# The first token block in another order, with one mask load and products split into a high and a low step

## The chip, the cores and the metric

The kernel runs on one NeuronCore of a Trainium2 chip. The metric is the device time of one execution in microseconds (us), the median of several runs. The engines go by their names in the trace: PE is TensorE (matmuls and transposes), PEld its weight loads, ACT is ScalarE, DVE is VectorE, POOL is GpSimd, and SP is SyncE, which here only issues DMAs. Each engine executes its instructions in the order in which they were written, so an instruction that waits holds up all that stand behind it.

## The reference

Windowed attention is followed by two feed-forward stages, all in float32:

```
scores = scale * q @ k.T                  # 4 batches, 8 heads, 576 positions, 64 per head
mask = (rel >= 0) & (rel < 64)            # a window of 64 positions back
attn = exp(scores - max) / (sum + 1e-9)
x = (attn @ v)                            # as 2304 tokens x 512
h = x @ w_in;  g = relu(h) ** 2;  x = g @ w_out        # 512 -> 2048 -> 512
y = ((x @ w_a) * (x @ w_b)) @ w_out2                   # 512 -> 1536 -> 512
```

## The kernel before

**Numbers in two parts.** A float32 operand is split into a high part (`hi`, `xh`, `wh`, rounded to the format FP32R) and a low part (`lo`, `xl`, `wl`, what the rounding left). A product is then three matmuls, high with high, high with low and low with high, which `mm3` issues one after another for each of the four slices of the contraction.

**Weights.** The weights arrive as 64-bit words. `conv` turns one tile of 128 x 512 into `wh` and `wl`: a load on SP (`raw`, two buffers), three passes on ACT (`a`, `s`, `wh`; lines 203, 208, 230) and four on DVE (lines 211, 218, 223, 233). A unit of the first feed-forward stage is 128 of its 2048 hidden features and needs one tile of `w_in` and one of `w_out`; below they are called i0, o0 to i6, o6 for the seven units of the first pass (`G1[0]`).

**Attention.** A chunk is 128 tokens. Its steps are scores on PE (`S`), maximum on DVE (`M`, `nm`), exponential on ACT (`E`, four instructions for each half chunk), normalisation on DVE (`N`, `p`), transposes on PE (`Tr`, `ps_p`), their copy on ACT (`pT`), values on PE (`V`, `ps_o`), and the split of the result into `xh` on ACT and `xl` on DVE. For the first five chunks the mask is added on PE, by a matmul with the identity (`ident_bf`, `mask_bf`) ahead of the scores; the later ones add it on DVE from `mask_sb`. The mask has three variants: the usual one, and two for a chunk that holds the start of a batch in its first or second half.

**A unit.** `unit1` projects a block of tokens (`H`, tile `ps_in`, 12 matmuls), forms `r`, `hi` and `g` on ACT (in the first block; later `g` is on DVE) and `lo` on DVE, and adds the product with `w_out` into four accumulators (`O`, tile `acc`, 12 matmuls). The first block of 512 tokens is four chunks. In its first pass, three units are computed in halves of 256 tokens and four whole.

**What sets the order.** All steps are put in a `Plan` with an engine, an assumed cost, their dependences and a rank. `Plan.issue` walks through assumed time and takes on each engine, among the steps that are ready within 0.15 us of the first, the one of lowest rank; the program is then written in that order. A rank is given by the order of the calls `attention`, `tiles` (a pair of `conv`) and `unit1` at the end of the kernel.

Of the kernel before, what the change touches and what calls it, by code (L numbers as in the profile page):

```python
# [8 lines left out]
F32 = mybir.dt.float32  # L9
# [20 lines left out]
G2 = [range(0, 6), range(6, 12)]  # L30
C0 = 4
MASK_PE = 5
N0 = 3
NPR = NCH // 2
# [86 lines left out]
def kernel(  # L121
# [39 lines left out]
    mask_sb = mk_p.tile([P, 3, P], F32, name="mask_sb")  # L161
    mask_bf = mk_p.tile([P, 3, P], BF16, name="mask_bf")
    ident_bf = mk_p.tile([P, P], BF16, name="ident_bf")
# [133 lines left out]
    def a_scores(c):  # L297
        pool, tag = (ps_acc, "acc") if c < 2 else (ps_w, "w")
        on_pe = c < MASK_PE
        for j in range(2):  # L300
            ps = T["s", c, j] = pool.tile([P, NHP, P], F32, tag=tag, name="ps_s")
            if on_pe:
                m = mask_bf[:, mask_of(c)].unsqueeze(1).to_broadcast([P, NHP, P])
# [77 lines left out]
    def attention(c, rank):  # L381
# [8 lines left out]
        for j in range(2):  # L390
            ps = ("S", c) if c >= 2 and j else None
            add(("M", c, j), "DVE", 0.8 if on_pe else 1.45, f(a_max, j), [("S", c), old("Tr", j)], rank,
                give=None if on_pe else ps)
# [15 lines left out]
    def u_proj(name, key, t, cols):  # L409
# [3 lines left out]
        for kc in range(KC):  # L413
            c = slice(kc * P, (kc + 1) * P)
            mm3(ps, h_[:, c], l_[:, c], xh[t][:, kc, cols], xl[t][:, kc, cols], kc == 0, kc == KC - 1)

    def e_tile(tag, n, dt=F32):
        return e_p.tile([P, 512], dt, tag=tag, name=tag)[:, :n]
# [4 lines left out]
    def unit1(t, u, us, cols, rank):  # L423
# [16 lines left out]
        def g_():  # L440
            T["g", k] = e_tile("g", n)
            if t == 0 and part_1:
                nc.scalar.activation(out=T["g", k], in_=T["r", k], func=AF.Square)
# [7 lines left out]
        def lo_():  # L451
            T["lo", k] = e_tile("lo", n, F32R)
            nc.vector.tensor_tensor(out=T["lo", k], in0=T["g", k], in1=T["hi", k].bitcast(F32), op=ALU.subtract)  # L453

        def out_():
            if fresh:
# [6 lines left out]
        e = 0.12 + 0.001 * n  # L463
        add(("H", k), "PE", 12 * mm_cost(n), lambda: u_proj(("H", k), ("in", u), t, cols),
            [("wlo", i), *x, ("H", k - 1) if k else None], rank, take="w")
        add(("r", k), "ACT", e, r_, [("H", k), *back(k, "g", "hi")], rank, give=("H", k))
        add(("hi", k), "ACT", e, hi_, [("r", k), *back(k, "O")], rank)
        add(("g", k), "ACT" if t == 0 and part_1 else "DVE", e, g_, [("r", k), *back(k, "lo")], rank)
        add(("lo", k), "DVE", e, lo_, [("g", k), ("hi", k), *back(k, "O")], rank)
        add(("O", k), "PE", 12 * mm_cost(n), out_,  # L470
            [("lo", k), ("wlo", o), ("O", k - 1) if k else None, *(acc_free[0] if fresh else ())], rank + 1.5)
        last_use["in", u], last_use["out", u] = ("H", k), ("O", k)
# [123 lines left out]
    def c_mask():  # L596
        nc.scalar.dma_start(out=mask_sb, in_=mask.unsqueeze(1).to_broadcast([P, 3, P]))
        make_identity(nc, ident)

    def c_masks():  # L600

        nc.gpsimd.tensor_copy(out=ident_bf, in_=ident)
        for e in range(2):
            nc.gpsimd.memset(mask_sb[e * W:(e + 1) * W, 1 + e, :W], NEG / SCALE)
        nc.gpsimd.tensor_copy(out=mask_bf, in_=mask_sb)

    add("mask", "ACT", 0.6, c_mask, [], -3, size=0.2)
    add("masks", "POOL", 1.5, c_masks, ["mask"], -3)


# [15 lines left out]

    halves = [slice(0, 256), slice(256, 512)]
    first = G1[0]
    attention(0, nxt())
    attention(1, nxt())  # L630
    for u in range(N0):
        tiles(1, u, nxt())
        if u:
            attention(1 + u, nxt())
        unit1(0, first[u], first, halves[0], nxt())
    for u in range(N0):
        unit1(0, first[u], first, halves[1], nxt())
        if u < N0 - 1:
            tiles(1, N0 + u, nxt())
    c = C0  # L640
    for j, u in enumerate(first[N0:]):
        if N0 + j >= 2 * N0 - 1:
            tiles(1, u, rank[0] - 2)
        attention(c, nxt())
        c += 1
        unit1(0, u, first, slice(0, 512), nxt())

# [96 lines left out]
```

## Time and profile before

| what | us |
|---|---|
| median of 3 runs (lowest, highest) | 942.81 (942.37, 943.44) |
| the profiled execution, its own time | 942.02 |
| its span, first to last instruction | 940.1 |
| PE busy in the span | 912.2 (97%) |
| DVE, ACT busy | 443.4, 384.5 |

The span is what the trace covers; the 1.9 us beside it lie outside the program's instructions. Of PE's idle time, 940.1 - 912.2 = 27.9 us, most lies in the first 62 us.

### The profile page before, as it was taken

The page shows a single profiled execution, that of the slowest core. Times are in us where ns is not written, and L with a number is a line of the kernel's source. Part 1 is how long each engine was busy: PE and PEld are TensorE (multiplying, and loading weights), DVE is VectorE, ACT ScalarE, POOL GpSimd, SP SyncE. Part 2 cuts the span into 40 slices and gives each one's busy share as a digit, 9 for nine tenths or more (in the row PEclk, how much of TensorE's full clock was granted, in tenths as well). Part 3 has the DMA queues.
Part 4 walks back from the last instruction along what each step waited for, and adds up shares of the span by engine and source line. Part 5 has one row for each costly group of instructions (what it writes and reads, how often), then busy time and mean ns, then how long its engine had stood idle before and what let it go on. Part 6 is the DMA issues. An engine that isn't in the chain of part 4 may idle for free.

```text
span 940.1 us, 13461 instructions
## 1 busy us (share of the span) xinstructions
PE 912.2 (97%) x5386; PEld 764.8 (81%) x5386; DVE 443.4 (47%) x849; ACT 384.5 (41%) x882; POOL 2.0 (0%) x11
## 2 busy tenths in 40 slices
PE   5789999999999999999999999999999999999997
PEld 3678887787898888888898888888898888888887
DVE  3888856746887242425498421212168121212122
ACT  4898744636786232223377311212158111111111
POOL 0000000000000000000000000000000000000000
PEclk8999999999999999999999999999999999999999
DMA  8866733411656010100045210101036020202010
GB/s 259 264 209 202 230 108 116 154 67 60 218 181 199 28 45 1 45 1 12 29 153 172 73 45 1 46 1 45 1 118 186 33 90 1 90 1 89 1 58 33
DMA packets 43213, 86.12 MB, mean 92 GB/s; under 512 B 3600, under 2 KB 14224, under 8 KB 43152
## 3 DMA queue, kind: packets, MB, share of 16 engines
q1 hardware_dynamic: 42224, 84.82, 27.5%
q8 instruction: 42, 0.69, 0.3%
q10 hardware_dynamic: 928, 0.46, 0.2%
q14 instruction: 19, 0.16, 0.0%
HBM read 71.11 MB, written 14.16 MB: 91 GB/s over the span
## 4 chain that ended last, share of the span: by engine, by line
PE 89%; DVE 5%; ACT 3%; DMA 2%; issue 1%; ACTq 0%; DVEq 0%
PE acc L170 12%; PE acc L171 12%; PE acc L172 11%; PE ps_in L170 6%; PE ps_in L172 6%; PE ps_in L171 6%; PE ps_b L170 5%; PE ps_b L172 5%; PE ps_a L171 5%; PE ps_a L172 5%; PE ps_b L171 5%; PE ps_a L170 5%; ACT p L336 1%; PE ps_p L351 1%; DMA raw<-in_w_out_dram 1%; PE ps_o L364 1%
## 5 line engine op out<-in xcount | busy, mean ns | idle before, releaser
L545 DVE TENSOR_TENSOR g<-r,ps_b 128x512 f32<-128x512 f32 (+1 forms) x60 | 38.0, 633 | 247.3 <-PE ps_b L172 247.2
L549 ACT CAST hi<-g 128x512 fp32r<-128x512 f32 (+1 forms) x60 | 34.6, 578 | 243.6 <-DVE g L545 242.9
L170 PE MATMUL ps_in<-xh,wh 128*128 128x512 f32 (+1 forms) x332 | 122.0, 367 | 2.3 <-ACT xh L374 2.3
L170 PE MATMUL acc<-hi,wh 128*128 128x512 f32 (+1 forms) x332 | 122.0, 367 | 0.9 <-ACT hi L449 0.9
L171 PE MATMUL acc<-lo,wh 128*128 128x512 f32 (+1 forms) x332 | 120.7, 363 | 2.0 <-DVE lo L453 2.0
L171 PE MATMUL ps_in<-xl,wh 128*128 128x512 f32 (+1 forms) x332 | 120.6, 363 | 1.6 <-DVE xl L379 1.6
L172 PE MATMUL ps_in<-xh,wl 128*128 128x512 f32 (+1 forms) x332 | 120.3, 362 | 0.9 <-DVE wl L233 0.9
L172 PE MATMUL acc<-hi,wl 128*128 128x512 f32 (+1 forms) x332 | 120.2, 362 | 0.0
L453 DVE TENSOR_TENSOR lo<-g,hi 128x512 fp32r<-128x512 f32 (+1 forms) x83 | 51.3, 618 | 105.7 <-ACT hi L449 101.8
L449 ACT ACTIVATE hi<-r 128x512 fp32r<-128x512 f32 (+1 forms) x83 | 47.6, 574 | 122.5 <-PE acc L172 122.0
L170 PE MATMUL ps_b<-xh,wh 128*128 128x512 f32 (+1 forms) x240 | 88.4, 368 | 0.0
L171 PE MATMUL ps_a<-xl,wh 128*128 128x512 f32 (+1 forms) x240 | 88.3, 368 | 0.0
L171 PE MATMUL ps_b<-xl,wh 128*128 128x512 f32 (+1 forms) x240 | 88.3, 368 | 0.0
L170 PE MATMUL ps_a<-xh,wh 128*128 128x512 f32 (+1 forms) x240 | 88.3, 368 | 0.0
L172 PE MATMUL ps_b<-xh,wl 128*128 128x512 f32 (+1 forms) x240 | 88.3, 368 | 0.0
L172 PE MATMUL ps_a<-xh,wl 128*128 128x512 f32 (+1 forms) x240 | 88.3, 368 | 0.0
L170 PE MATMUL acc<-wh,hi 128*128 128x512 f32 x216 | 84.3, 390 | 1.0 <-ACT hi L549 1.0
L171 PE MATMUL acc<-wl,hi 128*128 128x512 f32 x216 | 84.2, 390 | 0.0
L172 PE MATMUL acc<-wh,lo 128*128 128x512 f32 x216 | 84.0, 389 | 0.0
L170 PEld LDWEIGHTS ps_in<-xh,wh 128*128 128x128 f32 x332 | 63.1, 190 | 12.2 <-ACT xh L374 2.6
L170 PEld LDWEIGHTS acc<-hi,wh 128*128 128x128 f32 x332 | 62.7, 189 | 12.3 <-issue 1.2
L171 PEld LDWEIGHTS acc<-lo,wh 128*128 128x128 f32 x332 | 62.8, 189 | 12.1 <-DVE lo L453 2.9
(63 smaller groups left out, 1450.7 us busy)
## 6 DMA issues: line engine op xcount, KB each, us to landing
raw<-in_w_out_dram SPq DMA_DIRECT2D x28, 512.0 KB, 3.9
q_sb<-in_qbd_dram SPq DMA_DIRECT2D x18, 512.0 KB, 6.0
part<-ev SPq DMA_DIRECT2D x34, 256.0 KB, 2.6
pr<-part SPq DMA_DIRECT2D x34, 256.0 KB, 4.1
raw<-in_w_in_dram SPq DMA_DIRECT2D x16, 512.0 KB, 3.5
v_sb<-in_vwin_dram SPq DMA_DIRECT2D x14, 512.0 KB, 4.0
k_sb<-in_kT_dram SPq DMA_DIRECT2D x17, 384.0 KB, 4.8
raw<-in_w_a_dram SPq DMA_DIRECT2D x12, 512.0 KB, 3.6
```

The lines of the kernel that those rows point to most:

```text
L170: nc.tensor.matmul(ps, ah, bh, start=first, stop=False)
L171: nc.tensor.matmul(ps, ah, bl, start=False, stop=False)
L172: nc.tensor.matmul(ps, al, bh, start=False, stop=last)
L336: nc.scalar.activation(out=T["p", c, j][:, hp, :], in_=T["s", c, j][:, hp, :], func=AF.Exp, bias=T["nm", c, j][:, hp:hp + 1], scale=SCALE, ...
L351: nc.tensor.transpose(ps[:, hp, :], T["p", c, j][:, hp, :], ident)
L364: nc.tensor.matmul(ps[j * W:(j + 1) * W, hp, o], T["v", c][:, e, h * D:(h + 1) * D], T["pT", c, j][:, hp, o], start=True, stop=True,)
L449: nc.scalar.activation(out=T["hi", k], in_=T["r", k], func=AF.Square)
L453: nc.vector.tensor_tensor(out=T["lo", k], in0=T["g", k], in1=T["hi", k].bitcast(F32), op=ALU.subtract)
L545: nc.vector.tensor_tensor(out=T["g", k], in0=T["r", k], in1=T["B", k], op=ALU.mult)
L549: nc.scalar.copy(out=T["hi", k], in_=T["g", k])
```

## The change

The order of the first block is written as a string, `START`: `p0` is attention of chunk 0, `i0` and `o0` are the conversions of the two weight tiles of unit 0, `a0` and `b0` are the two halves of unit 0, and `f3` is unit 3 whole. Each word gets the next rank; before, the two tiles of a unit shared one. The mask is loaded once (64 KB, where 192 KB were loaded in three copies) and POOL makes the variants in three tiles of their own; the float32 variants for DVE are a later step, `masks_2`. In the first block's first pass `H` and `O` become two steps each in the plan: first the eight matmuls with the activation's high part, then the four with its low part. The number of matmuls is the same.

```diff
-C0 = 4
+START = "i0 o0 p0 p1 p2 a0 p3 a1 a2 b0 b1 i1 o1 i2 o2 i3 o3 b2 p4 i4 o4 p5 f3 i5 f4 f5 o5 p6 i6 p7 f6 o6"
-N0 = 3
...
+    def u_high(name, key, t, cols):
+
+        n = cols.stop - cols.start
+        ps = T[name] = ps_w.tile([P, 512], F32, tag="w", name=f"ps_{key[0]}")[:, :n]
+        for kc in range(KC):
+            c = slice(kc * P, (kc + 1) * P)
+            nc.tensor.matmul(ps, T["wh", key][:, c], xh[t][:, kc, cols], start=kc == 0, stop=False)
+            nc.tensor.matmul(ps, T["wl", key][:, c], xh[t][:, kc, cols], start=False, stop=False)
...
+        early = t == 0 and part_1
...
+        if early:
+            add(("H", k, 0), "PE", 8 * mm_cost(n), lambda: u_high(("H", k), ("in", u), t, cols),
+                [("wlo", i), *[("xh", c) for _, c in x], ("H", k - 1) if k else None], rank, take="w")
+            add(("H", k), "PE", 4 * mm_cost(n), lambda: u_low(("H", k), ("in", u), t, cols), [("H", k, 0), *x], rank)
...
+        if early:
+            add(("O", k, 0), "PE", 8 * mm_cost(n), out_high, [("hi", k), *before], rank + 1.5)
+            add(("O", k), "PE", 4 * mm_cost(n), out_low, [("lo", k), ("O", k, 0)], rank + 1.5)
...
     def c_mask():
-        nc.scalar.dma_start(out=mask_sb, in_=mask.unsqueeze(1).to_broadcast([P, 3, P]))
+        nc.scalar.dma_start(out=mask_sb[:, 0], in_=mask)
         make_identity(nc, ident)
+        nc.gpsimd.tensor_copy(out=ident_bf, in_=ident)
...
+        for v in (1, 0, 2):
+            nc.gpsimd.tensor_copy(out=mask_bf[v], in_=mask_sb[:, 0])
+            if v:
+                nc.gpsimd.memset(mask_bf[v][(v - 1) * W:v * W, :W], NEG / SCALE)
+
+    def c_masks_2():
+        for v in (1, 2):
+            nc.gpsimd.tensor_copy(out=mask_sb[:, v], in_=mask_sb[:, 0])
+            nc.gpsimd.memset(mask_sb[(v - 1) * W:v * W, v, :W], NEG / SCALE)
...
-    attention(0, nxt())
-    attention(1, nxt())
-    for u in range(N0):
...
+    for w in START.split():
+        what, x = w[0], int(w[1:])
+        if what == "p":
+            attention(x, nxt())
+        elif what in "io":
+            conv(({"i": "in", "o": "out"}[what], first[x]), nxt())
+        else:
+            unit1(0, first[x], first, halves[what], nxt())
```

What the new order makes of the program is shown at three places.

The first place is the start of ACT's instructions, up to the first exponentials (`p,rs`), before:

```order
1 L597 DMA mask_sb<-in_mask_dram 128x3x128
2 L276 DMA k_sb<-in_kT_dram 128x4x128
3 L336 ACT_TABLE_LOAD
4 L336 ACTIVATE p,rs<-ps_s,nm 128x128 x8
5 L203 ACTIVATE a<-raw 128x512
```

and now:

```order
1 L640 DMA mask_sb<-in_mask_dram 128x128
2 L275 DMA k_sb<-in_kT_dram 128x4x128
3 L202 ACT_TABLE_LOAD
4 L202 ACTIVATE a<-raw 128x512
5 L207 ACTIVATE s<-raw 128x512
6 L229 CAST wh<-a 128x512
7 L202 ACTIVATE a<-raw 128x512
8 L207 ACTIVATE s<-raw 128x512
9 L229 CAST wh<-a 128x512
10 L335 ACTIVATE p,rs<-ps_s,nm 128x128 x8
```

The two tiles of unit 0 are converted ahead of the first exponentials, and the load of the activation table stands ahead of both; it waited for `nm` of DVE and now waits for nothing. On DVE the matching eight passes stand ahead of the first maximum in the same way, and the first two loads of SP are these two tiles, ahead of `q` and `k` of the first chunks.

The second place is ACT where the second chunk's result is split (`xh`), before:

```order
13 L203 ACTIVATE a<-raw 128x512
14 L208 ACTIVATE s<-raw 128x512
15 L230 CAST wh<-a 128x512 x2
16 L374 CAST xh_91<-ps_o 128x4x128
17 L336 ACTIVATE p,rs<-ps_s,nm 128x128 x4
```

and now:

```order
19 L202 ACTIVATE a<-raw 128x512
20 L207 ACTIVATE s<-raw 128x512
21 L229 CAST wh<-a 128x512
22 L335 ACTIVATE p,rs<-ps_s,nm 128x128 x4
23 L373 CAST xh_91<-ps_o 128x4x128
24 L335 ACTIVATE p,rs<-ps_s,nm 128x128 x4
```

The four exponentials of the third chunk's first half have moved ahead of `xh`, on which the first projection on PE waits. The conversions here are those of unit 1, where before they were those of unit 0.

The third place is PE at the first accumulation, half unit `a0` into `acc`. Before, the matmul with `lo` was the second row of twelve:

```order
32 L170 MATMUL acc<-hi,wh 128x256
33 L171 MATMUL acc<-lo,wh 128x256
34 L172 MATMUL acc<-hi,wl 128x256
```

Now the eight matmuls with `hi` are followed by the eight of the next half unit with `xh`, and then by the four with `lo` and the four with `xl`; the last rows of each eight and what follows:

```order
42 L478 MATMUL acc<-hi,wh 128x256
43 L479 MATMUL acc<-hi,wl 128x256
44 L422 MATMUL ps_in<-xh_91,wh 128x256
45 L423 MATMUL ps_in<-xh_91,wl 128x256
...
50 L422 MATMUL ps_in<-xh_91,wh 128x256
51 L423 MATMUL ps_in<-xh_91,wl 128x256
52 L484 MATMUL acc<-lo,wh 128x256 x4
53 L428 MATMUL ps_in<-xl_96,wh 128x256 x4
54 L363 MATMUL ps_o<-pT,v_sb 64x64 x16
```

Between a matmul with a high part and the first one with the low part of the same activation there are now other matmuls. From the second block on, PE's order is the same as before but for a few places in that block.

## Rows read from the trace of the kernel before

**Rows 1.** The page's first line.

```profile
span 940.1 us, 13461 instructions
```

**Rows 2.** Windows: stretch, length, busy us of each engine, granted clock, DMA share, GB/s.

```profile
0.00:26.98 26.98, 14.14 (x183) 10.36 (x183) 11.67 (x29) 13.95 (x45) 1.99 (x11) 0.87 0.82 263
26.98:33.30 6.32, 3.19 (x20) 2.60 (x21) 5.91 (x16) 5.96 (x19) 0.00 (x0) 1.00 0.90 315
33.30:36.70 3.40, 3.40 (x18) 3.40 (x18) 3.16 (x8) 3.13 (x10) 0.00 (x0) 0.50 0.69 253
36.70:62.00 25.30, 20.07 (x242) 17.16 (x242) 20.96 (x50) 22.44 (x68) 0.00 (x0) 1.00 0.74 240
...
62.00:100.00 38.00, 38.00 (x403) 31.09 (x402) 30.84 (x68) 31.82 (x98) 0.00 (x0) 1.00 0.60 193
```

**Rows 3.** PE's waits from 26 to 62 us: releaser, us in total, times, longest.

```profile
PE ps_in L170 <- ACT xh L374: 2.3, 2, 1.2
PE acc L171 <- DVE lo L453: 2.0, 3, 1.1
PE ps_in L171 <- DVE xl L379: 1.6, 2, 1.1
PE ps_p L351 <- DVE p L346: 1.4, 2, 1.1
PE acc L170 <- ACT hi L449: 0.9, 1, 0.9
PE ps_in L172 <- DVE wl L233: 0.9, 1, 0.9
PE ps_p L351 <- ACT s L208: 0.4, 1, 0.4
```

**Rows 4.** Timeline of the start: start, length, instruction, idle before it.

```profile
8.66 1.98 PE L309 MATMUL ps_s<-k_sb,q_sb 64*64 64x128 f32 x32 [1.53 <-DMA k_sb<-in_kT_dram]
...
10.67 0.69 DVE L328 TENSOR_REDUCE nm<-ps_s 128x4 f32<-128x512 f32 x1 [10.67 <-PE ps_s L309]
...
11.65 1.28 ACT L336 ACT_TABLE_LOAD   x1 [11.65 <-DVE nm L329]
...
12.94 0.37 ACT L336 ACTIVATE p<-ps_s,nm 128x128 f32<-128x128 f32 x1
...
14.89 0.69 DVE L346 TENSOR_TENSOR p<-p,ri 128x512 f32<-128x512 f32 x1
...
26.35 0.58 ACT L374 CAST xh<-ps_o 128x512 fp32r<-128x512 f32 x1
...
26.98 0.38 PE L170 MATMUL ps_in<-xh,wh 128*128 128x256 f32 x1 [1.24 <-ACT xh L374]
```

**Rows 5.** DMA, GB/s of each of the first 40 us.

```profile
GB/s 0 16 170 346 345 342 377 395 406 418 279 223 215 385 351 356 369 342 375 125 16 0 66 356 447 180 197 339 273 152 262 416 403 391 295 274 37 29 229 274
```

**Rows 6.** ACT's groups, 12 to 62 us: busy us, mean ns, idle before.

```profile
L336 ACT ACTIVATE p<-ps_s,nm 128x128 f32<-128x128 f32 x40 | 14.1, 371 | 0.6 <-DVE nm L329 0.6
...
L208 ACT ACTIVATE s<-raw 128x512 uint16<-128x512 uint32 x10 | 7.9, 789 | 0.0
L203 ACT ACTIVATE a<-raw 128x512 f32<-128x512 f32 x10 | 6.8, 678 | 0.4 <-DMA raw<-in_w_in_dram 0.3
L230 ACT CAST wh<-a 128x512 fp32r<-128x512 f32 x10 | 6.2, 618 | 1.6 <-DVE a L223 1.6
L355 ACT COPY pT<-ps_p 128x512 f32<-128x512 f32 x9 | 5.2, 578 | 2.0 <-PE ps_p L351 2.0
```

**Rows 7.** Windows, columns as in the second group: the first 6 us.

```profile
0.00:6.00 6.00, 0.00 (x0) 0.11 (x1) 0.00 (x0) 0.00 (x0) 1.92 (x11) 1.00 0.69 203
```

**Rows 8.** Landing times of the `raw` loads up to 70 us.

```profile
DMA to landing us min/median/max: 3.4/4.5/8.8
```

**Rows 9.** Timeline of ACT, the `r` of the sixth half unit (`b2`).

```profile
61.99 0.39 ACT L438 ACTIVATE r<-ps_in 128x256 f32<-128x256 f32 x1
```

**Rows 10.** Chain that ended last: a matmul of 512 columns, from start to next.

```profile
62.23 0.23 PE ps_in L170
```

More of the change, by code (lines that the diff above doesn't have):

```diff
@@ L161 @@
     mask_sb = mk_p.tile([P, 3, P], F32, name="mask_sb")
-    mask_bf = mk_p.tile([P, 3, P], BF16, name="mask_bf")
+    mask_bf = [mk_p.tile([P, P], BF16, name=f"mask_bf{v}") for v in range(3)]
     ident_bf = mk_p.tile([P, P], BF16, name="ident_bf")
@@ L302, in a_scores @@
             if on_pe:
[L303 removed]
+                m = mask_bf[mask_of(c)].unsqueeze(1).to_broadcast([P, NHP, P])
                 nc.tensor.matmul(ps, ident_bf, m, start=True, stop=True, skip_group_check=True)
@@ L391, in attention @@
             ps = ("S", c) if c >= 2 and j else None
-            add(("M", c, j), "DVE", 0.8 if on_pe else 1.45, f(a_max, j), [("S", c), old("Tr", j)], rank,
+            add(("M", c, j), "DVE", 0.8 if on_pe else 1.45, f(a_max, j), [("S", c), old("Tr", j), None if on_pe else "masks_2"], rank,
                 give=None if on_pe else ps)
@@ L415, in u_proj, with u_low @@
             mm3(ps, h_[:, c], l_[:, c], xh[t][:, kc, cols], xl[t][:, kc, cols], kc == 0, kc == KC - 1)
+    def u_high(name, key, t, cols):
[5 more added lines that the diff above has]
+            nc.tensor.matmul(ps, T["wl", key][:, c], xh[t][:, kc, cols], start=False, stop=False)
+    def u_low(name, key, t, cols):
+        for kc in range(KC):
+            c = slice(kc * P, (kc + 1) * P)
+            nc.tensor.matmul(
+                T[name], T["wh", key][:, c], xl[t][:, kc, cols], start=False, stop=kc == KC - 1
+            )
     def e_tile(tag, n, dt=F32):
@@ L441, in g_ @@
             T["g", k] = e_tile("g", n)
-            if t == 0 and part_1:
+            if early:
                 nc.scalar.activation(out=T["g", k], in_=T["r", k], func=AF.Square)
@@ L453, in lo_, with out_high, out_low @@
             nc.vector.tensor_tensor(out=T["lo", k], in0=T["g", k], in1=T["hi", k].bitcast(F32), op=ALU.subtract)
+        def out_high():
+            if fresh:
+                T["acc"] = [ps_acc.tile([P, 512], F32, tag="acc", name="acc") for _ in range(KC)]
+            key = ("out", u)
+            for m in range(KC):
+                c = slice(m * P, (m + 1) * P)
+                acc = T["acc"][m][:, cols]
+                nc.tensor.matmul(acc, T["wh", key][:, c], T["hi", k], start=fresh, stop=False)
+                nc.tensor.matmul(acc, T["wl", key][:, c], T["hi", k], start=False, stop=False)
+        def out_low():
+            for m in range(KC):
+                c = slice(m * P, (m + 1) * P)
+                nc.tensor.matmul(
+                    T["acc"][m][:, cols], T["wh", ("out", u)][:, c], T["lo", k], start=False, stop=last
+                )
         def out_():
@@ L596, in c_mask @@
     def c_mask():
-        nc.scalar.dma_start(out=mask_sb, in_=mask.unsqueeze(1).to_broadcast([P, 3, P]))
+        nc.scalar.dma_start(out=mask_sb[:, 0], in_=mask)
         make_identity(nc, ident)
+        nc.gpsimd.tensor_copy(out=ident_bf, in_=ident)
     def c_masks():
[L602 to L608, printed above, removed]
+        for v in (1, 0, 2):
[6 more added lines that the diff above has]
+            nc.gpsimd.memset(mask_sb[(v - 1) * W:v * W, v, :W], NEG / SCALE)
+    add("mask", "ACT", 0.6, c_mask, [], -3, size=0.07)
+    add("masks", "POOL", 0.6, c_masks, ["mask"], -3)
+    add("masks_2", "POOL", 1.5, c_masks_2, ["masks"], -3)
     rank = [0]
@@ L625, in conv_ahead @@
             tiles(*todo_conv.pop(0), r)
-    halves = [slice(0, 256), slice(256, 512)]
+    halves = {"a": slice(0, 256), "b": slice(256, 512), "f": slice(0, 512)}
     first = G1[0]
-    attention(0, nxt())
-    attention(1, nxt())
-    for u in range(N0):
[L632 to L646, printed above, removed]
+    for w in START.split():
[4 more added lines that the diff above has]
+            conv(({"i": "in", "o": "out"}[what], first[x]), nxt())
+        else:
+            unit1(0, first[x], first, halves[what], nxt())
     def close():
```

15 lines of the change are left out of this document (9 added, 6 removed).

## The prediction

> **What bounds the kernel now.** I read the page first. Of a span of 940.1 us [rows 1] PE is busy for 912.2, so PE's own work is nearly the whole time. The change adds no matmul, and from the second block on PE's order hardly differs. Only time in which PE stands still, or runs slowly, can be won or lost. The windows say where that is [rows 2]. Up to the first projection, at 26.98 us, PE is busy for 14.14 us and idle for 12.8. From there to 62 us it is idle for 3.1 + 0.0 + 5.2 = 8.3 us. From 62 to 100 us it is busy for 38.00 of 38.00: there PE is the bound. So the kernel has a start of 62 us in which other engines feed PE too slowly, and about 21 us of idle time in it. In that start the granted clock also falls to 0.50 (1.2 GHz) for the 3.4 us from 33.3 on, after a stretch in which PE was busy for half the time [rows 2]. A product that takes 3.4 us there takes half at the other level, so that fall costs at most 1.7 us.
>
> The waits of PE say who is late after the first projection [rows 3]: `xh` and `xl` of a chunk, `lo` and `hi` of a unit, the normalised `p` ahead of its transposes, `wl` of a tile. They add up to 9.5 us, of which 1.24 is the wait that ends at the first projection [rows 4]; the other 8.3 are the idle time of the windows. They are all outputs of ACT and DVE. ACT is busy for 22.44 of the 25.30 us from 36.7 on, DVE for 20.96 [rows 2], so ACT is the engine that is behind.
>
> **The change part by part.** *The start.* Before, ACT did nothing until DVE had the first maximum: its table load began at 11.65, 1.28 us long, and the first exponential at 12.94 [rows 4]. Now the table load waits for nothing and ends long before. In its place the two tiles of unit 0 stand ahead of the first exponentials on ACT and ahead of the first maximum on DVE. When do they end? By the rates of each us [rows 5] 0.6 MB (one tile of 0.52 and the mask) have moved at 4.2 us; with 0.4 for landing the first tile is there at 4.6. A tile then goes through `a`, `s` and `wh` on ACT, 0.68 + 0.79 + 0.62 [rows 6], with two VectorE passes between and behind them, which I count as 0.7 each from the pass of the same size [rows 4]. The second tile's `a` follows the first's `wh`. That is about 2.8 us for the first tile up to `wh` and 3.4 for the second up to `wl`, so DVE is free for the maximum at 10.8.
>
> The scores may be late too, since SP's first loads are now the two tiles. They need at least tiles, `q`, `k` and mask, 1.05 + 0.52 + 0.26 + 0.07 = 1.9 MB, which had moved at 7.8 us; if `k` lands only after `k` and `q` of the second chunk as well, it is 2.8 MB, 10.0 us [rows 5]. Before, the scores began at 8.66, with 2.3 MB moved, of which 1.8 were SP's; by the same 1.8 MB of SP beside ACT's smaller 0.33 it is 8.3. I take that. Scores of 2.0 us then end at 10.3, DVE starts at 10.8, and after 0.98 us (10.67 to 11.65 before) the first exponential starts at 11.8. The gain is 1.1 us, with bounds of 1.1 and -0.2 (scores from 10.1, exponential at 13.1).
>
> *The first projection.* It waits for `xh` of the second chunk, at 26.35 [rows 4]. The four exponentials that now stand ahead of it take 1.4 us (14.1 for 40 [rows 6]). So the first projection comes at 26.98 - 1.1 + 1.4 = 27.3: a loss of 0.3.
>
> *After it.* The split lets PE do eight other matmuls while `lo` or `xl` is made, so 2.0 + 1.6 go. Conversions that were done earlier take away the wait for `wl`, 0.9; `hi` and one `xh` are awaited under transposes and scores, 0.9 and 1.1; the waits of the transposes are 1.4 + 0.4. All of these are 8.3. From laying out the printed order with the durations above I expect these to be there in their place, as estimates. The transposes of the third chunk come before its normalisation: 0.4. Those of the fourth chunk wait because its eight exponentials (2.8 us) and its normalisation (about 1.1) now follow in one piece: 0.6. The tile of `o3` can be loaded only when `s` of `o2`, two tiles earlier, has been read. ACT has some 3.5 us of work before it wants the tile, and a load lands in 3.4 to 4.5 us, 8.8 at worst [rows 8]: 0.7. The transposes of the sixth chunk come behind the `r` of the first whole unit: 0.7. And 0.5 for what such a layout does not see. Together 2.9. Between nothing and all of the 8.3 again I take this, since each has its place.
>
> *The clock.* Between the second values and the first projection there is still a gap, so I count half of the 1.7 us as won, 0.85.
>
> *The sum by PE:* 8.3 - 2.9 - 0.3 + 0.85 = 6.0 us.
>
> *The sum by ACT* is a second way. Up to the `r` of the sixth half unit, at 61.99 [rows 9], ACT converted ten tiles [rows 6], now six between the first exponential and that `r`, and it copies `pT` eight times for nine. Consecutive activations overlap (40 of 371 ns are 14.8, busy 14.1 [rows 6]), so I count a tile as 1.9, not 2.09. The `r` then comes at 61.99 - 1.1 - 4 x 1.9 - 0.6 = 52.7. Two of the four tiles are only put off; what ACT has won at equal work is 1.1 + 2 x 1.9 = 4.9 us. I take 5.5, between the two.
>
> *The mask.* POOL gets its 64 KB earlier than 192 KB, but PE's first mask matmul then only stands longer before the scores, which wait for `k`: nothing won. If `k` were there at once, up to 2 us of the mask would count. POOL now works from about 4.3 us, where DVE has its conversion passes. Before, POOL's 1.92 us lay in the first 6 us, in which DVE did nothing [rows 7], so no row shows the two together. Five of POOL's new instructions read the tiles; at the mean of 1.92/11 = 0.17 us they can hold up DVE by 0.9 us, or by nothing. I take nothing and keep the 0.9 for the range.
>
> The Trainium skill, "SBUF — State Buffer", section "Who interferes with whom", states that a VectorE instruction with two SBUF inputs and a GpSimd instruction that reads SBUF lock each other out for the whole instruction. No run so far shows it here; by that rule the sum would be up to 0.9 us lower, by the row it stays.
>
> **The rivals.** *1. The start is late.* The scores wait for 2.8 MB, or POOL holds up DVE. The first exponential comes at 12.7 to 13.1 and the gain falls by 0.9 to 1.3, to about 4.3: 938.5 us. For it speaks that the tiles are ahead of `q` on SP's queue; against it that ACT's queue carries `k`.
>
> *2. The waits come back.* Every wait that goes is traded for another: the exponentials of two half chunks in one piece hold up `r` on ACT, the tiles of units 4 to 6, which now come later, hold up the whole units, and the 2.9 us become 7 or 8. Then it is 942 to 943. For it speaks that ACT's work as a whole stays the same and that it was behind; against it that ACT had 11.65 us of nothing to do at the start, which now hold two tiles.
>
> *3. Slower: `r` waits.* The end of a projection now lies behind eight matmuls of the unit before it. At 0.23 us for a matmul of 512 columns [rows 10] these are 0.9 us for a half unit and 1.8 for a whole one; with the four low ones, 1.4 and 2.8. If ACT comes to `r` before that end, it stands, and everything behind `r` in its queue with it. For ten units (six halves, four whole) at 0.9 and 1.8 this is 12.6 us, and the time 942.8 - 5.5 + 12.6 = 950. It decides from 5.5 us on, a little over half a us for each `r`. In the layout ACT comes to `r` after the end each time, since it is the engine that is behind; this speaks against it.
>
> **How the numbers follow.** The profiled execution took 942.02 us, 0.8 below the median of 942.81, which is also what the change will be measured by. 942.02 - 5.5 = 936.5 for a profiled execution; on the scale of the medians 942.8 - 5.5 = 937.3. I give this case 0.66, rival 1 0.12, rival 2 0.12, rival 3 0.10. About 0.2% (1.9 us) is what a measurement of this kernel can tell from no change; the forecast and rival 1 are on the faster side, 0.78, rival 2 within it, 0.12, rival 3 slower, 0.10. The range starts where nearly all of the 8.3 and the clock's 1.7 are won, with the start's 0.3 lost (9.7, so 933.1; I say 933.0), and ends where rival 1 has 2.5 us of further waits, 941.0. That leaves out rival 3 and most of rival 2. The likeliest case's own range is 934.5 to 939.5.
>
> **What would show it.** In the changed profile the table load stands before 4 us and the first exponential at 11.8; the first projection at about 27.3; `r` of the sixth half unit between 52 and 54. PE's waits for `lo` and `xl` are gone or under 0.5 in total, and PE's idle time between the first projection and 62 us is about 3 us, not 8.3. Wrong would be a first exponential after 13, ACT waiting for `ps_in` before `r` by more than 3 us in total, or new waits of PE for `wl` or `p` of more than 4.

## The result, and the profile after

| | before | after |
|---|---|---|
| median of 4 runs (lowest, highest), us | 943.12 (942.37, 944.33) | 931.97 (930.90, 932.50) |
| the profiled execution, us | 942.02 | 932.39 |
| its span, us | 940.1 | 930.7 |
| PE busy, us | 912.2 | 911.0 |

The ratio is 0.9878, with a 95% interval of 0.9866 to 0.9891: 11.15 us faster by the medians, 9.6 by the profiled executions. The sign was forecast, the size was not: 937.3 was the forecast, and the result lies 1 us below the range. The first rows of the page after:

```profile
span 930.7 us, 13470 instructions
...
PE 911.0 (98%) x5386; PEld 764.3 (82%) x5386; DVE 444.3 (48%) x849; ACT 384.2 (41%) x882; POOL 3.7 (0%) x17
```

The windows after, in the columns and stretches of [rows 2]:

```profile
0.00:26.98 26.98, 15.05 (x182) 10.80 (x182) 16.97 (x40) 18.42 (x59) 3.67 (x17) 0.87 0.89 297
26.98:33.30 6.32, 6.19 (x60) 5.57 (x61) 5.02 (x14) 4.79 (x17) 0.00 (x0) 0.73 0.75 284
33.30:36.70 3.40, 3.40 (x53) 3.23 (x51) 2.88 (x9) 3.40 (x19) 0.00 (x0) 1.00 0.83 265
36.70:62.00 25.30, 24.83 (x278) 22.19 (x274) 21.86 (x49) 23.93 (x69) 0.00 (x0) 1.00 0.73 243
62.00:100.00 38.00, 37.13 (x391) 29.51 (x390) 33.95 (x74) 32.79 (x97) 0.00 (x0) 1.00 0.68 213
```

PE's waits after, from 26 to 62 us, beside the seven of [rows 3]. The first ends at the first projection:

```profile
PE ps_in L422 <- ACT xh L373: 2.0, 1, 2.0
PE ps_p L350 <- DVE p L345: 0.5, 1, 0.5
```

The timeline after, with the rows that answer to [rows 4] and [rows 9] (start, length, instruction, idle before it):

```profile
1.84 1.28 ACT L202 ACT_TABLE_LOAD   x1 [1.84 <-issue]
...
4.58 0.67 ACT L202 ACTIVATE a<-raw 128x512 f32<-128x512 f32 x1 [1.45 <-DMA raw<-in_w_in_dram]
...
8.51 1.99 PE L308 MATMUL ps_s<-k_sb,q_sb 64*64 64x128 f32 x32 [2.05 <-DMA k_sb<-in_kT_dram]
...
10.54 0.68 DVE L327 TENSOR_REDUCE nm<-ps_s 128x4 f32<-128x512 f32 x1
...
11.53 0.37 ACT L335 ACTIVATE p<-ps_s,nm 128x128 f32<-128x128 f32 x1 [1.63 <-DVE nm L328]
...
27.11 0.56 PE L422 MATMUL ps_in<-xh,wh 128*128 128x256 f32 x1 [2.01 <-ACT xh L373]
...
51.83 0.39 ACT L454 ACTIVATE r<-ps_in 128x256 f32<-128x256 f32 x1
```

What the reader is to see: the first projection comes no earlier (26.98, now 27.11), so the start wins nothing for PE. From there to 62 us PE was idle for 8.4 us and is idle for 0.5. From 62 to 100 us it had no idle time and has 0.9 now. All is won before the second block's first result: the first stores of the second and the third block (`part`) stand at 143.56 and 196.51 us, where they stood at 153.21 and 206.19, 9.65 and 9.68 earlier.

The span's 9.4 us by PE's idle and busy time, each entry from the windows, the page and the start of the first projection:

| PE, us | before | after | won | forecast |
|---|---|---|---|---|
| idle up to the first projection | 12.84 | 12.06 | 0.8 | |
| idle from there to 62 us | 8.36 | 0.47 | 7.9 | |
| idle from 62 to 100 us | 0.00 | 0.87 | -0.9 | |
| idle later | 6.68 | 6.32 | 0.4 | |
| idle after the first projection, sum | 15.04 | 7.66 | **7.4** | 5.4 |
| busy up to 26.98 us | 14.14 | 15.05 | -0.9 | |
| busy later | 898.1 | 895.9 | **2.15** | 0.85 (the clock) |
| start of the first projection | 26.98 | 27.11 | **-0.13** | -0.3 |

The three entries in bold add up to 9.4; the forecast's to 6.0, of which 5.5 was taken.

### The profile page after: what moved, and what is told of

Read it like the earlier page. It is cut to its first block, busy times and chain, and to the rows that moved or that the text cites. A ratio compares the mean times of both kernels' runs of the same rounds, so it can differ in the third digit from the quotient of the medians.

```text
span 930.7 us, 13470 instructions
## 1 busy us (share of the span) xinstructions
PE 911.0 (98%) x5386; PEld 764.3 (82%) x5386; DVE 444.3 (48%) x849; ACT 384.2 (41%) x882; POOL 3.7 (0%) x17
## 4 chain that ended last, share of the span: by engine, by line
PE 93%; DVE 3%; ACT 3%; issue 0%; DMA 0%; DVEq 0%; ACTq 0%
PE acc L169 11%; PE acc L170 11%; PE acc L171 11%; PE ps_in L169 6%; PE ps_in L170 6%; PE ps_in L171 6%; PE ps_b L171 5%; PE ps_a L170 5%; PE ps_a L171 5%; PE ps_b L170 5%; PE ps_a L169 5%; PE ps_b L169 5%; PE ps_p L350 2%; ACT p L335 2%; PE ps_o L363 1%; PE ps_s L308 1%
## 5 line engine op out<-in xcount | busy, mean ns | idle before, releaser
L169 PE MATMUL acc<-hi,wh 128*128 128x512 f32 (+1 forms) x292 | 108.2, 370 | 0.0
L169 PE MATMUL ps_in<-xh,wh 128*128 128x512 f32 (+1 forms) x292 | 108.0, 370 | 0.0
L170 PE MATMUL acc<-lo,wh 128*128 128x512 f32 (+1 forms) x292 | 107.0, 367 | 0.0
L170 PE MATMUL ps_in<-xl,wh 128*128 128x512 f32 (+1 forms) x292 | 106.9, 366 | 0.0
L171 PE MATMUL ps_in<-xh,wl 128*128 128x512 f32 (+1 forms) x292 | 106.9, 366 | 0.0
L171 PE MATMUL acc<-hi,wl 128*128 128x512 f32 (+1 forms) x292 | 106.9, 366 | 0.0
L169 PEld LDWEIGHTS acc<-hi,wh 128*128 128x128 f32 x292 | 55.1, 189 | 10.0 <-issue 0.9
L169 PEld LDWEIGHTS ps_in<-xh,wh 128*128 128x128 f32 x292 | 55.0, 189 | 9.4 <-ACT r L454 0.2
L171 PEld LDWEIGHTS acc<-hi,wl 128*128 128x128 f32 x292 | 55.1, 189 | 9.2
```

What stands on the lines that cost most here:

```text
L169: nc.tensor.matmul(ps, ah, bh, start=first, stop=False)
L170: nc.tensor.matmul(ps, ah, bl, start=False, stop=False)
L171: nc.tensor.matmul(ps, al, bh, start=False, stop=last)
```

## The experiments

| kernel | median, us | ratio to before, 95% interval |
|---|---|---|
| the changed kernel | 931.97 | 0.9878 [0.9866, 0.9891] |
| `tiles_first` | 938.66 | 0.9949 [0.9934, 0.9964] |
| `late_tiles` | 943.32 | 0.9996 [0.9983, 1.0009] |
| `order_only` | 945.65 | 1.0025 [1.0015, 1.0034] |
| `split_only` | 949.35 | 1.0061 [1.0045, 1.0077] |
| `same_order_no_split` | 940.71 | 0.9970 [0.9959, 0.9981] |
| `join_f4` | 934.95 | 0.9908 [0.9893, 0.9923] |
| `join_but_f4` | 936.81 | 0.9930 [0.9915, 0.9945] |
| `join_out` | 935.17 | 0.9916 [0.9901, 0.9932] |
| `join_filled` | 938.56 | 0.9949 [0.9932, 0.9966] |
| `join_half` | 933.09 | 0.9890 [0.9874, 0.9906] |
| `join_whole` | 940.21 | 0.9964 [0.9952, 0.9976] |
| `mask3` | 932.40 | 0.9884 [0.9870, 0.9898] |
| `keep_busy` | 933.33 | 0.9892 [0.9879, 0.9906] |
| `keep_busy2` | 931.43 | 0.9872 [0.9858, 0.9886] |

The medians of the kernel before in these comparisons were 943.1 to 943.5.

### Parts of the change alone

**`tiles_first`** is the kernel before with the two tiles of unit 0 ranked ahead of the first two chunks, and nothing else.

```diff
+    tiles(1, 0, nxt())
     attention(0, nxt())
     attention(1, nxt())
     for u in range(N0):
-        tiles(1, u, nxt())
+        if u:
+            tiles(1, u, nxt())
         if u:
             attention(1 + u, nxt())
```

> The kernel before, with one line moved: the two weight tiles of unit 0 are ranked ahead of the first two chunks, so that ACT and DVE convert them before the first exponential and the table load waits for nothing. No split of the products, three copies of the mask as before. Theory A (the gain comes from the work that ACT and DVE get done in the empty start): most of the 11 us appear, 934 to 936 us, the first exponential at 11.5 to 12. Theory B (the gain comes from the high products that cover PE's waits for lo and xl): at most the 1.3 us of the earlier exponential, 941 to 942 us, and PE still waits 3 us or more for lo and xl.

It took 938.66, 4.7 us less than the kernel before and between its two expectations. The table load moves to 1.91 us and the first exponential to 11.85 (1.84 and 11.53 in the changed kernel), and PE's waits from 26 to 62 us shrink, but do not go:

```profile
PE ps_in L170 <- ACT xh L374: 3.9, 2, 2.3
PE ps_p L351 <- DVE p L346: 2.4, 1, 2.4
PE ps_in L171 <- DVE xl L379: 0.7, 2, 0.3
PE acc L171 <- DVE lo L453: 0.2, 1, 0.2
```

Without any split the waits for `lo` and `xl` are 0.9 us where they were 3.6 [rows 3]: with two tiles out of ACT's and DVE's way these come in time. The 4.7 us are near the 4.9 that the prediction's sum by ACT gave for work done in the empty start.

**`late_tiles`** is the changed kernel with the two tiles behind the first two chunks.

```diff
-START = "i0 o0 p0 p1 p2 a0 ...
+START = "p0 p1 i0 o0 p2 a0 ...
```

> The changed kernel with i0 and o0 behind p0 and p1 in the order; all else is kept, the split too. Theory A: the table load waits for the maximum again, ACT is idle until 12.9 and the two tiles stand in the busy stretch; the loss is what ACT had won, 1.1 + 3.8 = 4.9 us or more: 937 to 940 us. Theory B: the products stay split and PE's waits for lo and xl stay covered, so that little is lost: 932 to 934 us.

943.32, no change against before, and above both expectations. The first exponential is at 10.56 here and the first projection at 25.17, 1.9 us earlier than in the changed kernel, and yet nothing is won: PE waits for 7.2 us from 26 to 62 us. The early tiles cost time up to the first projection and save more than that behind it.

**`order_only`** has the changed kernel's string and mask, but joined products; **`split_only`** has the old order, the split products and the single mask. In both the planner places every step anew.

```diff
 order_only, against the changed kernel, for H and for O:
-        if early:
+        if False:
```

> The changed kernel without the split: H and O are one step of twelve matmuls each, in the old order within them. The order of the first block and the single mask load are kept. Theory A: only the waits for lo and xl come back, one at a time: 933 to 935 us. Theory B: PE's waits for lo and xl come back with 3.6 us and the tails around them: 936 to 939 us.

> The order of the first block as in the kernel before, with the products in two steps and the single mask load as in the changed one. Theory A: ACT is as late as before, so PE finds little to put under its waits: 940 to 943 us. Theory B: the waits for lo and xl go, 3.6 us and more: 936 to 939 us.

Both are slower than before, by 2.3 and 6.0 us, and above all their expectations. In `order_only` PE waits once for `ri` of a normalisation, for 5.7 us. In `split_only` PE is busy for 6.40 of the 10 us from 50 on, at a mean clock of 0.66, as this row of its windows shows:

```profile
50.00:60.00 10.00, 6.40 (x32) 5.85 (x32) 7.94 (x19) 8.56 (x25) 0.00 (x0) 0.66 0.82 281
```

So the parts cannot be added up: early tiles alone win 4.7, order and split alone lose, all together win 11. Each of these four kernels also got another order from the planner, and so they say little on the split itself. The next kernels therefore keep the written order.

### The split, with the order kept

**`same_order_no_split`** has the changed kernel's order of all steps, but each unit's eight matmuls with the high part are moved directly ahead of its four with the low part.

```diff
+        seq = [i for _, _, i in sorted(order)]
+        key = lambda i: self.steps[i][0]
+        for i in [i for i in seq if len(key(i)) == 3 and key(i)[0] in ("H", "O") and key(i)[2] == 0]:
+            seq.remove(i)
+            seq.insert(seq.index(self.at[key(i)[:2]]), i)
-        for _, _, i in sorted(order):
+        for i in seq:
```

> The changed kernel with its written order kept step for step, but with the eight matmuls with a high part moved directly ahead of the four with the low part of the same step, so that H and O are again twelve matmuls in one piece. Nothing is planned anew. Theory A (the split matters only through the order that the planner makes of it): lo and xl are ready in most places by the time PE comes there, so 0 to 2 us are lost, 932 to 934 us. Theory B (the products put between are the cover): the waits for lo and xl return with 3 us or more, 935 to 938 us.

940.71, above both expectations: the split is worth 8.7 us in this order, against products joined at the place of their low part. But not where the prediction had it. `r` of the sixth half unit comes at 52.01 (51.83 with the split). Some of that is luck: the granted clock ahead of the first projection is higher here (a mean of 0.79 from 16 to 24 us, 0.57 in the changed kernel), and the projection starts at 26.35 and not at 27.11. From it to that `r` it takes 25.66 us, where the changed kernel takes 24.72 (and 25.22 and 25.37 in `mask3` and `keep_busy` below, which keep its order): at most 0.9 is lost there. No wait for `lo` stands in the first 100 us. The large loss comes at the second whole unit, f4, whose `r` comes at 74.96 and not at 69.26. PE's timeline there, first of the changed kernel:

```profile
59.13 1.15 PE L363 MATMUL ps_o<-pT,v_sb 128*64 128x64 f32 x32
60.22 0.51 PE L422 MATMUL ps_in<-xh,wh 128*128 128x512 f32 x1
...
61.96 0.40 PE L423 MATMUL ps_in<-xh,wl 128*128 128x512 f32 x1
62.27 0.63 PE L350 MATMUL ps_p<-ident,p 128*128 128x128 f32 x4
63.63 0.63 PE L350 MATMUL ps_p<-ident,p 128*128 128x128 f32 x4 [0.73 <-DVE p L345]
```

and of `same_order_no_split`:

```profile
59.34 1.15 PE L368 MATMUL ps_o<-pT,v_sb 128*64 128x64 f32 x32
62.50 0.63 PE L355 MATMUL ps_p<-ident,p 128*128 128x128 f32 x4 [2.01 <-ACT p L340]
63.86 0.66 PE L355 MATMUL ps_p<-ident,p 128*128 128x128 f32 x4 [0.73 <-DVE p L350]
65.05 2.45 PE L368 MATMUL ps_o<-pT,v_sb 128*64 128x64 f32 x32 [0.52 <-ACT pT L359]
67.42 0.80 PE L483 MATMUL acc<-hi,wh 128*128 128x512 f32 x1
68.02 0.63 PE L484 MATMUL acc<-hi,wl 128*128 128x512 f32 x1
```

In the changed kernel f4's eight matmuls with `xh` (60.22 to 62.27) stand between the values of one chunk and the transposes of the next. Without them PE waits there for exponentials and `p`. Behind the wait the granted clock falls to 0.50 (1.2 GHz): the values take 2.45 us for 1.15, matmuls start 0.43 apart and not 0.23. The windows of 59 to 65 us of the changed kernel, and of 59 to 65 and 65 to 71 us of this one:

```profile
59.00:65.00 6.00, 5.27 (x53) 4.11 (x53) 5.79 (x15) 5.88 (x19) 0.00 (x0) 1.00 0.69 258
```

```profile
59.00:65.00 6.00, 2.78 (x42) 1.85 (x40) 5.79 (x15) 5.88 (x20) 0.00 (x0) 0.94 0.71 269
65.00:71.00 6.00, 5.95 (x40) 4.89 (x41) 4.70 (x9) 3.99 (x7) 0.00 (x0) 0.50 0.53 151
```

DVE and ACT are busy for as long in the first six us as in the changed kernel (5.79 and 5.88), so PE's 2.5 us less are simply lost. ACT then stands 5.8 us before f4's `r`.

From this I formed the theory that the split gives PE something to do where it would wait for the attention (filler), against the prediction's that it covers the making of `lo` and `xl` (cover). Six kernels test it, all by the edit above with another condition on the unit:

```diff
+ join_f4:     key(i) == ("H", 7, 0)               # the projection of f4 alone
+ join_but_f4: ... and key(i) != ("H", 7, 0)       # all but that
+ join_out:    key(i)[0] == "O" and key(i)[2] == 0 # the accumulations alone
+ join_half:   ... and key(i)[1] <= 5              # the six half units alone
+ join_whole:  ... and key(i)[1] > 5               # the four whole units alone
```

> The changed kernel with the split taken back in the six half units alone: there the eight matmuls with hi or xh stand directly ahead of the four with lo or xl; the four whole units keep theirs in two places. Filler theory, in the form that the last four runs leave: the split is worth nothing before 59 us, since r of the sixth half unit came at 51.5 to 52.4 in every kernel of this series; the time is within 1 us of the changed kernel's 932.4. Cover theory, as the prediction had it: the waits for lo and xl that were counted (3.6 us) lay in the half units, so 935 to 936 and r of the sixth half unit 2 us or more later.

> The complement: the split taken back in the four whole units alone. Filler theory: this carries all of the 8.7 us, 939.5 to 941.5, with PE's waits at 60 to 64 us (some 2.7 us) and at 86 to 97 us (some 2.7 us) back. Cover theory: 935.5 to 937, since only the waits of whole units come back.

These two decide. `join_half` took 933.09, `join_whole` 940.21, where the kernel with all joined took 940.71: the split is worth 8.2 us in the four whole units, and 1.1 in the half units, which the intervals do not tell from nothing. Its trace says the same: from the first projection to the sixth `r` it takes 25.65 us, 0.9 more than the changed kernel. The windows from 60 to 80 and from 80 to 100 us, of `join_half`, then of `join_whole`, and the second of the two of the changed kernel:

```profile
60.00:80.00 20.00, 19.27 (x196) 14.93 (x195) 18.66 (x41) 19.03 (x55) 0.00 (x0) 1.00 0.65 237
80.00:100.00 20.00, 19.85 (x205) 15.91 (x203) 17.51 (x39) 15.59 (x50) 0.00 (x0) 1.00 0.69 214
```

```profile
60.00:80.00 20.00, 18.11 (x124) 14.25 (x124) 13.92 (x33) 14.46 (x42) 0.00 (x0) 0.83 0.54 187
80.00:100.00 20.00, 17.30 (x190) 13.95 (x189) 15.70 (x36) 16.04 (x50) 0.00 (x0) 1.00 0.59 174
```

```profile
80.00:100.00 20.00, 19.86 (x229) 16.00 (x228) 17.51 (x38) 15.97 (x55) 0.00 (x0) 1.00 0.73 218
```

There are two places, then: one at 60 to 64 us with a fall of the clock behind it, and one between 80 and 100 us, where PE of `join_whole` is idle for 2.7 us and that of the changed kernel for 0.1.

> The changed kernel with one edit on PE: the eight matmuls of the projection of f4 with xh no longer stand ahead of the transposes of the chunk p5, but directly ahead of their four with xl, behind the accumulation of f3; every other row stands where it was. Filler theory: what the split is worth lies in places where PE would wait for something else than lo or xl. At 60.2 to 62.3 us in the changed kernel these eight matmuls stand where PE would otherwise wait for the exponentials and the p of that chunk (waits of 2.0, 0.7 and 0.5 us in the kernel with all products joined), after which the granted clock falls to 0.50. By it this one place carries most of the 8.7 us that the split is worth with the order fixed: PE waits at 60 to 63 us again, r of f4 comes at 73 to 75 instead of 69.3, and the time is 936 to 939. Cover theory: the split is worth the waits for lo and xl, in many places and little in each. By it this kernel loses at most the eight matmuls once, under 1.5 us, and takes 932 to 933.7.

> The complement: in the changed kernel the high eight of every unit's projection and accumulation in the first block stand directly ahead of their low four, only f4's projection keeps its two places. Filler theory: the wait for the chunk p5 at 60 to 63 us is filled as in the changed kernel and the clock holds there, so most of the 8.7 us stays won: 933.5 to 936.5, r of f4 at 69 to 71. Cover theory: waits for lo and xl stand in all other units, 938.5 to 940.7, near the kernel with all joined.

934.95 and 936.81. The first is 1 us under what the filler theory gave and 1.3 over what the cover theory gave; the second is 0.3 over the one and 1.7 under the other. In `join_f4` the waits of 2.0 and 0.7 us are back and f4's `r` is at 72.54, but from 80 us on PE is busy for 19.84 of 20 us: it loses only the first place. In `join_but_f4` the clock holds at 1.00 from 60 to 80 us and `r` is at 70.72, but the second place is lost (17.31 of 20 us busy). So f4's projection carries 3 to 4 us, not most of the 8.7.

> The changed kernel with only the accumulations joined: their eight matmuls with hi stand directly ahead of their four with lo, projections keep their two places. Filler theory: the projections do nearly all of it; the waits for lo that come back are those of half units, one or two us: 932.5 to 934.5. Cover theory: lo and xl count alike, so this is about half of the 8.7 us: 935.5 to 937.5, with 2 us or more of PE's waits for lo.

935.17, between the two expectations: accumulations carry some 3 us, more than the filler theory said, yet no wait for `lo` is among PE's, which the cover theory wanted to be 2 us. PE idles 1.4 and 1.3 us at the two places. The eight matmuls with `hi` are such a filler as well.

**What these kernels leave open.** All of them join a product at the place of its low part, where the low part has been made; so none of them could have shown the waits for `lo` and `xl` that the cover theory speaks of. Joined at the place of the high part instead, no kernel was run, and for the whole units the changed kernel's trace speaks for this rival:

```profile
42.16 0.69 DVE L378 TENSOR_TENSOR xl<-ps_o,xh 128x512 fp32r<-128x512 f32 x1 [0.26 <-ACT xh L373]
```

```profile
64.01 0.68 DVE L469 TENSOR_TENSOR lo<-g,hi 128x512 fp32r<-128x512 f32 x1
64.02 0.47 PE L478 MATMUL acc<-hi,wh 128*128 128x512 f32 x1
...
65.71 0.39 PE L479 MATMUL acc<-hi,wl 128*128 128x512 f32 x1
```

The `xl` at 42.16 is that of the first block's last chunk, 13 us ahead of the first whole unit's projection (55.80). The `lo` of f3 is made at 64.69, before its eight matmuls with `hi` end; for f4 to f6 it is made at 72.63, 78.24 and 88.99, and the eight end at 74.2, 79.5 and 89.9. In all four whole units the four low matmuls could thus have followed the eight without a wait. What is shown there is what it is worth that eight matmuls of a product come early. That the product has to be in two steps for it is not shown.

### The clock

**`join_filled`** is the kernel with all joined, with eleven useless matmuls in f4's gap.

```diff
     def a_transpose(c, j):
+        if c == 5:
+            busy(ps, 3 if j else 8)      # identity by identity, 512 columns, overwritten
```

> The kernel with all products joined (940.7 us), with eleven added matmuls whose result is thrown away (identity by identity, 512 columns, bfloat16, overwritten by the transposes): eight ahead of the first four transposes of chunk p5 and three ahead of the second four, where PE waits there. Nothing of the computation is left out. They change no wait of the order, only whether PE is busy before 65 us. Clock theory: of what f4's r comes late (5.7 us) some 2.9 us are the clock: values that took 2.45 us at 0.50 instead of 1.15, and eight matmuls 0.43 apart instead of 0.23. With the fill the clock holds, r of f4 comes at 71.5 to 72.5 instead of 75.0 and the time is 937 to 938.5. Rival: the clock is of no weight, since ACT and DVE set the end of that stretch: r of f4 comes earlier, but the time stays within 1 us of 940.7.

938.56, 2.15 us less than without them. The intervals of the two ratios touch (0.9966 and 0.9959 at their near ends), but no run of the one reached the times of the other (938.94 at most, 939.25 at least), and the trace shows the gain in its place. The added matmuls bring no work forward, they only fill:

```profile
60.85 1.90 PE L304 MATMUL ps_p<-ident_bf 128*128 128x512 bf16 x8
62.92 0.63 PE L362 MATMUL ps_p<-ident,p 128*128 128x128 f32 x4 [0.17 <-ACT p L345]
...
65.95 1.15 PE L375 MATMUL ps_o<-pT,v_sb 128*64 128x64 f32 x30 [0.15 <-ACT pT L366]
```

The clock stays at 1.00, the values take 1.15 us again, f4's projection starts at 69.89 for 72.02 (2.13 earlier), and `r` is at 72.81, a little later than expected (71.5 to 72.5). So of the split's 8.7 us about 2 are the clock; the rival, that the clock has no weight here, falls.

**`keep_busy`** and **`keep_busy2`** put such matmuls into the start of the changed kernel: nine between the first chunk's two mask matmuls, ahead of its scores, five and four ahead of the first chunk's transposes, and in `keep_busy2` seven more ahead of the first projection.

```diff
+            if c == 0 and j:
+                busy(ps, 9)
...
+        if c == 0:
+            busy(ps, 5 - j)
...
+        if name == ("H", 0):              # keep_busy2 alone
+            busy(full..., 7)
```

> As the run with added matmuls in four places, but without the seven ahead of the first projection. By the clock theory the first fall of the clock goes, the second stays: 930 to 931.5 us; by the rival 931.5 to 933 us.

> The changed kernel with matmuls added on PE that compute nothing of use (identity by identity, into PSUM tiles that are written anew afterwards): 9 between the first two mask matmuls, 5 and 4 ahead of the first chunk's transposes, 7 ahead of the first projection. They stand where PE waits for others. If the low granted clock from about 17 to 24 us and 27 to 30.5 us costs time on the path: the clock stays at full, the first projection comes at 25 to 26 instead of 27.1 and the whole at 928.5 to 930.5 us. If ACT and DVE set the pace there, or the added matmuls hold up what follows them: 931.5 to 934 us.

933.33, above both its expectations, and 931.43; the intervals of both overlap that of the changed kernel. In `keep_busy2` the clock is 1.00 in all of the first 100 us, the first projection comes at 26.25 and `r` of the sixth half unit at 49.96, 1.9 us earlier; of this 1.2 are left in the span. PE then waits for `p` at 36.01, 60.96 and 62.32 us. Where ACT and DVE are behind, a faster PE waits longer for them. `keep_busy` lost its gain in the start: its nine added matmuls took 4.05 us and held up the first scores to 10.25 us (8.51 in the changed kernel), and the first exponential came at 12.40, 0.9 later.

### The mask

**`mask3`** is the changed kernel with the mask loaded in three copies, as before; POOL's part is unchanged.

```diff
-        nc.scalar.dma_start(out=mask_sb[:, 0], in_=mask)
+        nc.scalar.dma_start(out=mask_sb, in_=mask.unsqueeze(1).to_broadcast([P, 3, P]))
```

> The changed kernel with the mask loaded in three copies (192 KB) as before; the variants are made by GpSimd as in the changed one, from the first copy. If the mask is hidden behind the load of k, as the prediction has it: 932 us, within 1. If the 128 KB more delay k and the weight tiles and so the first exponential: 0.4 us later there, 932.5 to 933.5.

932.40, the same within the intervals. The scores start 0.4 us later (8.95), the first exponential comes at 11.95 and the first projection at 27.52. That cannot be put down to the mask: in the kernels above that have the changed kernel's start with its one mask, the scores begin between 8.55 (`join_filled`) and 9.02 (`join_half`).

## Why the prediction was right in sign and wrong in size

**Right: the start.** Scores were forecast at 8.3 and came at 8.51, DVE's first maximum at 10.8 (10.54), the first exponential at 11.8 (11.53), the first projection at 27.3 (27.11). The early tiles pay behind the first projection, not ahead of it.

**Right: the lock of POOL and DVE at nothing.** POOL's copies from 4.79 us on lie beside DVE's passes of the first tile:

```profile
4.58 0.47 DVE L210 TENSOR_SCALAR s<-raw 128x512 uint16<-128x512 uint16 x1 [4.58 <-DMA raw<-in_w_in_dram]
...
4.79 0.40 POOL L647 CAST mask_bf<-mask_sb 128x128 bf16<-128x128 f32 x1 [2.88 <-DMA mask_sb<-in_mask_dram]
...
5.33 0.76 POOL L647 CAST mask_bf<-mask_sb 128x128 bf16<-128x128 f32 x2
...
5.95 0.69 DVE L222 CUSTOM_DVE_ANT_0 a<-a,s 128x1024 uint16<-128x1024 uint16 x1 [0.24 <-ACT s L207]
...
6.36 0.43 POOL L653 COPY mask_sb<-mask_sb 128x128 f32<-128x128 f32 x1
6.56 0.54 DVE L210 TENSOR_SCALAR s<-raw 128x512 uint16<-128x512 uint16 x1
...
8.56 0.69 DVE L222 CUSTOM_DVE_ANT_0 a<-a,s 128x1024 uint16<-128x1024 uint16 x1 [0.21 <-ACT s L207]
```

The pass with two inputs at 5.95 takes 0.69 us beside the copies that end at 6.09 and start at 6.36, which it overlaps in part, and 0.69 for the second tile at 8.56, when POOL is done. The pass at 6.56, with one input, takes 0.54; its median over the first 12 tiles is 0.47. That is 0.1 us in all. The price that was kept for the range, 0.9 us for five copies, was too low in itself: the five took 0.37 to 0.43 us each, not 0.17, but held up nothing. The rule of the Trainium skill ("SBUF — State Buffer", "Who interferes with whom"), that such a pass and POOL's reads lock each other out, shows no cost for that pass here; what it would cost where both run for long, no run here shows.

**Right: `lo`, `xl`, `wl` and `hi` are no longer waited for.** But the reason given for the first two, that the split covers them, is not what the runs showed: `tiles_first` takes 3.6 us of them down to 0.9 with no split at all, and `join_half`, which takes the split back in the six half units, loses 1.1 us at most.

**Wrong, the step that failed: the 2.9 us of remaining waits.** 1.3 us came, 0.47 up to 62 us and 0.87 from there to 100. All but 0.14 of it are the waits given to the fourth and to the sixth chunk's transposes (forecast 0.6 and 0.7, measured 0.47 and, in the row at 63.63 us, 0.73). The third chunk's transposes (0.4), the tile of `o3` (0.7) and the unseen (0.5) cost PE nothing. With 0.4 us won later, which the sum did not have, PE's idle time after the first projection fell by 7.4 and not 5.4.

**Wrong, the mechanism of the split.** It was credited with 3.6 us of cover for `lo` and `xl` in the half units, and with nothing behind 62 us, where PE had been the bound [rows 2]. In the half units the two steps earn 1.1 us at most; in the whole units the early eight matmuls earn 8.2, as a filler of waits for attention behind 59 us. PE comes to the whole units earlier than before (f3's `r` at 59.84 us, 65.91 before), and the exponentials and `p` of the chunks between them are then what is late: `join_whole` shows a good part of rival 2, the waits coming back, and ends at 940.21. The changed kernel puts eight matmuls of a whole unit into such places. Rival 2 was weighed at 0.12 without asking which row would stand in the place where it would strike.

**Wrong: the mean of two sums.** The sum by ACT, 4.9, is what `tiles_first` wins, 4.7. It leaves out all that the split fills, so it was no second estimate of the same thing, and drawing the forecast from 6.0 to 5.5 moved it the wrong way. Its `r` of the sixth half unit was nearly right, though: 52.7, measured 51.83.

**Wrong: the clock's 0.85 us.** The stretch at 0.50 is not gone, only earlier: the mean of 0.73 over the 6.32 us from 26.98 on is 3.4 us at 0.50, as long as before [rows 2]. So the 2.15 us by which PE's busy time fell after the first projection have another reason. The trace before offers one, in the rows behind a wait:

```profile
28.44 0.39 PE L171 MATMUL ps_in<-xl,wh 128*128 128x256 f32 x1 [1.08 <-DVE xl L379]
28.66 0.28 PE L172 MATMUL ps_in<-xh,wl 128*128 128x256 f32 x1
28.78 0.27 PE L170 MATMUL ps_in<-xh,wh 128*128 128x256 f32 x1
```

In a row of matmuls the next starts after 0.12 us. Behind a wait it starts after 0.22, and ahead of a wait the last is counted with its whole 0.28. A stop so costs 0.26 us of busy time, and between the first projection and 100 us PE stopped 11 times before and stops three times now: 2.1 us. This is an estimate, and no run tests it. The 0.9 us more ahead of the first projection fit the clock: its mean from 16 to 24 us is 0.57 in both, but PE is busy for 7.37 us of them and not 6.54, since the third chunk's scores now fall into it and take 1.85 us for 1.10.

**Rivals 1 and 3** did not come. ACT waits for `ps_in` before `r` by 1.5 us in all from 20 to 100 us, the longest 1.1; with all products joined it is 8.0.

The sum, then: 5.5 + 0.5 (the mean) + 2.0 (idle) + 1.3 (busy) + 0.2 (start) = 9.5, which is the span's 9.4 but for rounding; the profiled executions differ by 9.6. The other 1.5 us up to the medians are how those two executions lie in their runs: before 1.1 under its median, after 0.4 over it. No trace explains these 1.5 us. The lower end of the range, 933.0, stood for 9.7 us won: the profiled executions, with 9.6, lie just inside it, the medians 1 us outside. What the terms above explain is why the forecast was 4 us short.

## What to carry to other kernels

When an early wait is removed, PE reaches later stages sooner, and the next late engine is to be looked for in a stretch that now shows no wait at all: a row "38.00 of 38.00" is a statement on the old order only. A long product with a part that is ready early is worth starting early where that part can fill a gap of another stage; here this was worth more than the wait between its two parts. Whether it has to be in two steps for that is to be asked by itself: no run here did. And a part of a change is to be undone with the written order kept; where a planner orders anew, the run measures the planner as well.

## What the runs showed of the hardware that had not been expected

- A wait of 2.0 and one of 0.7 us of PE, close together, were followed by about 6 us at a granted clock of 0.50 (the window of 65 to 71 us) in `same_order_no_split`; in `join_f4`, after the same two waits, by 3.4. Eleven useless matmuls in the gap of the former kernel kept it at 1.00 and won 2.15 us in time, in a stretch where PE was the bound. The same means in the start, where ACT and DVE were behind, moved the sixth `r` by 1.9 us and the time by 0.5 (931.97, 931.43), which their intervals do not tell apart.
- POOL's copies beside DVE's passes cost DVE about 0.1 us in all, and DVE's pass with two inputs took as long beside them as without them (0.69 us).
- Moving ACT's table load of 1.28 us into the empty start needed no edit of its own: it goes ahead of the first activation, whichever it is. Where that is a pass over a tile, the load started at 1.84 us, before the tile was there (4.58); where it is the exponential, the load started only with `nm` (9.27 us in `late_tiles`, 11.65 before [rows 4]).
